# Twenty subtractions between two layers: who makes them, and when

## The chip, the cores and the metric

The kernel runs on one core of one Trainium2 chip. The metric is the device time of one execution in microseconds; a kernel's time is the median of its runs. The core's engines work side by side, each through its own queue in order, and wait for each other by semaphores: TensorE (PE; PEld is its weight load), VectorE (DVE), ScalarE (ACT), GpSimd (POOL), and SyncE (SP), which issues the transfers.

## The reference, cut to what matters

Attention with two kinds of windows makes x (2304 tokens by 512), and two layers follow:

```python
def _moe_ref(x, w_gate, w_val, w_out):       # first layer, inner width 1536
    g = x @ w_gate
    silu = g * (1.0 / (1.0 + np.exp(-g)))
    val = x @ w_val
    return (silu * val @ w_out).astype(np.float32)

def _moe2_ref(x, w1, w2, w3, w_out):         # second layer, inner width 1024
    a = x @ w1
    b = x @ w2
    h = a * b @ w3
    return (h @ w_out).astype(np.float32)
```

The weights come as 64-bit floats. The output of the first layer is the x of the second, and the change is about that hand-over.

## The kernel before

Every product is made from two parts of each operand. A float32 value v is split into hi, its rounding to float32r, and lo = v - hi; a product is then three matmuls (hi hi, hi lo, lo hi). For x these are the tiles `x_hi` and `x_lo`, one of each per group of tokens, with the 512 rows of x in four parts of 128 (kk, or cc where they are written). The 2304 tokens are five groups g = 0 to 4: four of 512 and a short one of 256.

After the attention stage the program is a list of 100 steps (c, g): chunks c = 0 to 11 are the first layer (128 inner columns each), c = 12 to 19 the second, and in each chunk the five groups follow one another. The order of a step is the order of the code, on every engine:

- `up_mm(c, g)` (L540): TensorE makes pa and then pb, 12 matmuls each, two products of x with the chunk's weights. `up_product` (L526) puts the matmuls that read `x_lo` at places 3, 7, 11 and 12 of the twelve; the last reads part 3 of `x_lo`.
- `up_act` (L557): ScalarE makes ga from pa (silu in the first layer, a copy in the second), VectorE pr = pb * ga (L613), ScalarE sh, the hi part of pr (L620), GpSimd sl = pr - sh (L621).
- `down` of the step before (`down1` L703 for the first layer, `down2` L728 for the second): TensorE multiplies sh and sl of the previous step by the output weights, four results of three matmuls in four PSUM banks po0 to po3, and VectorE adds each to the running sum (y in the first layer, o in the second, L701; the first time it copies, L699). A bank's next use waits until VectorE has read it.
- for g = 4, from chunk 11 on, `fold_mm` (L750): 24 matmuls that multiply w3 by the output weights.
- the weight jobs of the step (`next_job`): VectorE turns 64-bit weights into float32 with five instructions (L125 to L135, the tiles val_w), for w3 also a transpose (L180); ScalarE takes the hi part (L191, for w3 L183, w3h) and GpSimd subtracts (L192, for w3 L184, w3l). Chunk 11 has jobs in steps (11,0) and (11,1), chunk 12 in (12,0) to (12,3): two of w3, then two of the next chunk's weights.

In chunk 11 `down1` finishes y, and there x for the second layer is made: after each addition ScalarE writes `x_hi` (L722), and a subtraction makes `x_lo` (L726), for parts 0 and 2 on GpSimd, for 1 and 3 on VectorE. Parts 0 to 2 are subtracted when the following part has been added. Both write with a stride, as the second layer takes the tokens in another order. The first reader of group g of these tiles is `up_mm(12, g)`; `down1(11, g)` is issued in the step behind (11, g), and `up_mm(12, g)` four steps later.

Before the list of steps, the attention stage runs with its own order; the change doesn't touch it.

Of the kernel before, what the change touches and what calls it, by code (L numbers as in the profile page):

```python
# [9 lines left out]
F32 = mybir.dt.float32  # L10
# [4 lines left out]
ALU = mybir.AluOpType  # L15
# [19 lines left out]
def attention_ffn_kernel(  # L35
# [14 lines left out]
    nc = tc.nc  # L50
# [4 lines left out]
    KT = DM // P  # L55
# [3 lines left out]
    NFT = FF // P  # L59
# [4 lines left out]
    groups = []  # L64
    t0 = 0
    while t0 < NT:
        n = min(512, NT - t0)
# [14 lines left out]
    def tokens(x, kk, t0, n):  # L82
        a = t0 - t0 % 512
        assert t0 + n <= a + 512
        return x[a // 512][:, kk, t0 - a:t0 - a + n]
# [20 lines left out]
    def bank(tag, name, bufs):  # L106
        return ps.tile([P, 512], F32, tag=tag, name=name, bufs=bufs)
# [88 lines left out]
    def jobs_of(c):  # L196

        res = [[] for _ in groups]
        if c + 1 < NCH:
            first = 1  # L200
            if c == NFT - 2:

                res[0].append(("w3", 0, 0))
                res[4].append(("w3", 0, 1))
            if c == NFT - 1:
                first = 0
            if NFT <= c:
                f = c + 1 - NFT
                res[0].append(("w3", f, 0))
                res[1].append(("w3", f, 1))  # L210
                first = 2
            if c == 0:

                res[4].append(("w", 1, 2))
            else:
                for j in range(3 if c + 1 < NFT else 2):
                    res[first + j].append(("w", c + 1, j))
        if 1 <= c <= NJ:
            res[4].append(("wo", c - 1, 0))
        return res  # L220
# [22 lines left out]
    def next_job():  # L243

        while not next(running):
            pass
# [279 lines left out]
    def up_product(c, g, j, pt):  # L526

        t0, n = groups[g]
        hi, lo = whl[c]

        terms = [(a, x, kk) for kk in range(KT) for a, x in ((hi, x_hi), (lo, x_hi))]
        for kk in range(KT):
            terms.insert(min(4 * kk + 2, len(terms)), (hi, x_lo, kk))
        for i, (a, x, kk) in enumerate(terms):
            ws = slice((j * KT + kk) * P, (j * KT + kk + 1) * P)
            nc.tensor.matmul(out=pt[:, :n], lhsT=a[:, ws], rhs=tokens(x, kk, t0, n),  # L536
                             start=i == 0, stop=i == len(terms) - 1)
            yield

    def up_mm(c, g):  # L540
        pa = bank("pa", f"pa{c}_{g}", 2)
        pb = bank("pb", f"pb{c}_{g}", 2)
        for j, pt in enumerate((pa, pb)):
            for _ in up_product(c, g, j, pt):
                pass
        upp[c, g] = pa, pb

    def up_gate(c, g, pa):
        n = groups[g][1]
        ga = sp.tile([P, 512], F32, tag="ga", name=f"ga{c}_{g}", bufs=2)  # L550
        if c < NFT:
            nc.scalar.activation(out=ga[:, :n], in_=pa[:, :n], func=AF.Silu)
        else:
            nc.scalar.copy(out=ga[:, :n], in_=pa[:, :n])
        return ga

    def up_act(c, g):  # L557
        pa, pb = upp.pop((c, g))
        up_val(c, g, up_gate(c, g, pa), pb)
# [50 lines left out]
    def up_val(c, g, ga, pb):  # L610
        n = groups[g][1]
        pr = sp.tile([P, 512], F32, tag="pr", name=f"pr{c}_{g}", bufs=2)
        nc.vector.tensor_tensor(out=pr[:, :n], in0=pb[:, :n], in1=ga[:, :n], op=ALU.mult)  # L613
        split_act(c, g, pr)
# [82 lines left out]
    def accumulate(dst, src, first):  # L697
        if first:
            nc.vector.tensor_copy(out=dst, in_=src)  # L699
        else:  # L700
            nc.vector.tensor_tensor(out=dst, in0=src, in1=dst, op=ALU.add)  # L701

    def down1(c, g):  # L703

        t0, n = groups[g]
        hi, lo = whl[c]
        sh, sl = st.pop((c, g))
        if c == 0:
            acc[g] = yp.tile([P, KT, n], F32, tag=f"acc{g}", name=f"y{g}")
        y = acc[g]  # L710
        rest = []
        for cc in range(KT):
            ws = slice(2 * PW + cc * P, 2 * PW + (cc + 1) * P)
            po = bank(f"po{cc}", f"po{c}_{g}_{cc}", 1)
            for a, x, first, last in ((hi, sh, True, False), (hi, sl, False, False), (lo, sh, False, True)):
                nc.tensor.matmul(out=po[:, :n], lhsT=a[:, ws], rhs=x[:, :n], start=first, stop=last)  # L716
            accumulate(y[:, cc, :], po[:, :n], c == 0)
            if c == NFT - 1:

                xh, xl = (tokens(x, cc, t0, n).rearrange("p (a m r) -> p a r m", m=QB, r=DIL) for x in (x_hi, x_lo))  # L720
                yc = y[:, cc, :].rearrange("p (a r m) -> p a r m", m=QB, r=DIL)
                nc.scalar.copy(out=xh, in_=yc)  # L722
                rest.append((cc, xl, yc, xh.bitcast(F32)))
            while rest and (cc == KT - 1 or rest[0][0] < cc):
                i, xl, yc, xh = rest.pop(0)
                (nc.vector if i % 2 else nc.gpsimd).tensor_tensor(out=xl, in0=yc, in1=xh, op=ALU.subtract)  # L726

    def down2(c, g):  # L728

# [16 lines left out]
    def down(c, g):  # L746
        (down1 if c < NFT else down2)(c, g)


    def fold_mm(f):  # L750
        pt = bank("pa", f"fold{f}", 2)
        for j in range(NJ):
            hi, lo = w3T[f, j // HJ]
            for a, b, first, last in ((hi, wo_hi, True, False), (hi, wo_lo, False, False), (lo, wo_hi, False, True)):
                nc.tensor.matmul(out=pt, lhsT=a[:, j % HJ * P:(j % HJ + 1) * P], rhs=b[:, j, :],  # L755
                                 start=first and j == 0, stop=last and j == NJ - 1)
        hi, lo = (t[:, 2 * PW:WC] for t in slice_tiles(NFT + f))
        nc.scalar.copy(out=hi, in_=pt)
        nc.vector.tensor_tensor(out=lo, in0=pt, in1=hi.bitcast(F32), op=ALU.subtract)

    for n, (c, g) in enumerate(steps):
        if n >= 2:
            if n >= GFILL:
                up_mm(c, g)
            up_act(c, g)
        if n >= 1:
            down(*steps[n - 1])
        f = c + 1 - NFT
        if 0 <= f < NF2:
            if g == 4:  # L770
                fold_mm(f)
        for _ in jobs_of(c)[g]:
            next_job()
# [31 lines left out]
```

## Time and profile before

| what | us |
|---|---|
| median of 3 runs | 884.83 (884.32 to 885.89) |
| the profiled execution | 883.91 |
| its span, first to last instruction | 882.1 |
| TensorE busy | 865.2 (98%) |
| VectorE busy | 605.6 (69%) |
| GpSimd busy | 300.5 (34%) |
| ScalarE busy | 249.7 (28%) |

All times in rows are microseconds from the start of the span. A windows row has, for one stretch, its length, then for PE, PEld, DVE, ACT and POOL the busy time and the number of instructions, then the granted TensorE clock as a share of full speed, the share of time that the DMA engines moved data, and GB/s. A timeline row has the start, the time taken, engine, line, operation, the tiles it writes and reads, shapes, and how many like instructions were merged into it; in brackets stands the time that the engine had been idle before it, and what ended that. Matmuls overlap in their pipeline, so their pace is read from start to start, not from the time that one takes. An instruction that is held up while it executes shows a longer time, not an idle one. A row of a line's summary gives the least, the median and the greatest time of one in ns. A chain row has start, time, engine, tile, line and count of merged instructions.

### The profile page before, as it was taken

How to read it: one execution, taken by the hardware profiler on the slowest of the kernel's cores; microseconds unless marked ns; L12 is line 12 of the kernel's file. 1: busy time of each engine (PE TensorE's matmuls, PEld its weight loads, DVE VectorE, ACT ScalarE, POOL GpSimd, SP SyncE). 2: the span in 40 equal slices, each digit the busy share in tenths (PEclk: the TensorE clock that was granted, in tenths of full speed). 3: DMA queues.
4: the chain of work that ended last, by engine and by line, in shares of the span. 5: the costliest groups of instructions: out<-in, count | busy, mean ns of one | idle time of the engine just before them, and what ended most of it. 6: DMA issues, size and time to landing. Idle time of an engine off the chain costs nothing.

```text
span 882.1 us, 13481 instructions
## 1 busy us (share of the span) xinstructions
PE 865.2 (98%) x5192; PEld 722.0 (82%) x5192; DVE 605.6 (69%) x1078; ACT 249.7 (28%) x503; POOL 300.5 (34%) x296
## 2 busy tenths in 40 slices
PE   8899999999999999999999999999999999999998
PEld 5678778888888888888888887888888888888886
DVE  6898876676766767666677766767574757575725
ACT  5788521212222112221122256212121212121211
POOL 7676522322323223232232354323131323131311
PEclk9999999999999999999999999999999999999999
DMA  7998401211212112121121220112121212120014
GB/s 190 228 178 195 124 28 45 72 49 48 71 48 72 49 48 72 48 72 48 48 72 38 69 61 1 50 47 60 37 68 45 55 50 63 32 73 25 1 48 166
DMA packets 105551, 61.70 MB, mean 70 GB/s; under 512 B 71696, under 2 KB 100624, under 8 KB 105488
## 3 DMA queue, kind: packets, MB, share of 16 engines
q1 hardware_dynamic: 104944, 60.58, 25.5%
q8 instruction: 41, 0.67, 0.3%
q10 hardware_dynamic: 544, 0.26, 0.1%
q14 instruction: 22, 0.18, 0.1%
HBM read 56.10 MB, written 4.72 MB: 69 GB/s over the span
## 4 chain that ended last, share of the span: by engine, by line
PE 86%; DVE 9%; ACT 2%; issue 1%; DMA 1%; POOL 1%; SPq 0%; DVEq 0%; ACTq 0%; POOLq 0%
PE pa L536 26%; PE pb L536 26%; PE po L716 15%; PE po L741 11%; PE fold L755 5%; DVE mx L442 1%; DVE s L436 1%; ACT x_hi L722 1%; DVE mx L452 1%; DMA raw_w<-in_moe_w_gate_dram 1%; DVE x_lo L726 1%; DVE x_lo L518 1%; PE pp L470 1%; PE av L500 1%; DVE val_w L132 1%
## 5 line engine op out<-in xcount | busy, mean ns | idle before, releaser
L613 DVE TENSOR_TENSOR pr<-pb,ga 128x512 f32<-128x512 f32 (+1 forms) x98 | 62.4, 637 | 206.0 <-PE pb L536 99.7
L621 POOL TENSOR_TENSOR sl<-pr,sh 128x512 fp32r<-128x512 f32 (+1 forms) x98 | 115.9, 1183 | 240.3 <-ACT sh L620 239.7
L536 PE MATMUL pa<-x_hi,whi 128*128 128x512 f32 (+1 forms) x392 | 143.7, 369 | 0.0
L536 PE MATMUL pa<-x_hi,wlo 128*128 128x512 f32 (+1 forms) x392 | 143.5, 368 | 0.0
L536 PE MATMUL pb<-x_hi,whi 128*128 128x512 f32 (+1 forms) x392 | 143.2, 367 | 0.0
L536 PE MATMUL pb<-x_hi,wlo 128*128 128x512 f32 (+1 forms) x392 | 143.2, 367 | 0.0
L192 POOL TENSOR_TENSOR wlo<-val_w,whi 128x512 fp32r<-128x512 f32 x52 | 67.3, 1294 | 193.4 <-ACT whi L191 193.3
L701 DVE TENSOR_TENSOR y<-po,y 128x512 f32<-128x512 f32 (+1 forms) x220 | 131.5, 632 | 0.0
L536 PE MATMUL pb<-x_lo,whi 128*128 128x512 f32 (+1 forms) x392 | 128.4, 368 | 0.0
L536 PE MATMUL pa<-x_lo,whi 128*128 128x512 f32 (+1 forms) x392 | 128.2, 368 | 0.0
L620 ACT CAST sh<-pr 128x512 fp32r<-128x512 f32 (+1 forms) x98 | 56.8, 580 | 149.3 <-DVE pr L613 145.8
L191 ACT CAST whi<-val_w 128x512 fp32r<-128x512 f32 x52 | 32.3, 622 | 227.1 <-DVE val_w L135 227.1
L716 PE MATMUL po<-sh,whi 128*128 128x512 f32 (+1 forms) x240 | 88.7, 369 | 1.4 <-DVE y L701 1.1
L716 PE MATMUL po<-sl,whi 128*128 128x512 f32 (+1 forms) x240 | 88.7, 369 | 1.4 <-POOL sl L621 1.4
L716 PE MATMUL po<-sh,wlo 128*128 128x512 f32 (+1 forms) x240 | 88.3, 368 | 0.0
L536 PEld LDWEIGHTS pa<-x_hi,whi 128*128 128x128 f32 x392 | 73.9, 188 | 12.7
L536 PEld LDWEIGHTS pa<-x_hi,wlo 128*128 128x128 f32 x392 | 73.9, 188 | 12.6
L536 PEld LDWEIGHTS pb<-x_hi,wlo 128*128 128x128 f32 x392 | 73.9, 189 | 12.2
L536 PEld LDWEIGHTS pb<-x_hi,whi 128*128 128x128 f32 x392 | 73.9, 189 | 12.2
L536 PEld LDWEIGHTS pa<-x_lo,whi 128*128 128x128 f32 x392 | 72.4, 188 | 12.4
L536 PEld LDWEIGHTS pb<-x_lo,whi 128*128 128x128 f32 x392 | 72.5, 189 | 12.1
L701 DVE TENSOR_TENSOR o<-po,o 128x512 f32<-128x512 f32 x126 | 81.3, 685 | 0.2 <-PE po L741 0.2
(108 smaller groups left out, 1351.9 us busy)
## 6 DMA issues: line engine op xcount, KB each, us to landing
raw_w<-in_moe_w_dram SPq DMA_DIRECT2D x256, 32.0 KB, 1.8
raw_w<-in_moe_w_dram SPq DMA_DIRECT2D x16, 512.0 KB, 3.5
raw_w<-in_moe_w_gate_dram SPq DMA_DIRECT2D x12, 512.0 KB, 3.7
raw_w<-in_moe_w_val_dram SPq DMA_DIRECT2D x12, 512.0 KB, 3.6
raw_w<-in_moe_w_out_dram SPq DMA_DIRECT2D x12, 512.0 KB, 3.5
out_dram<-o SPq DMA_DIRECT2D x18, 256.0 KB, 2.1
raw_wo<-in_moe_w_out_dram SPq DMA_DIRECT2D x8, 512.0 KB, 3.5
vnear<-in_v_dram SPq DMA_DIRECT2D x32, 96.0 KB, 4.4
```

The source lines that it names most:

```text
L132: nc.vector.scalar_tensor_tensor(out=b, in0=up, scalar=-0x40000000, in1=b, op0=ALU.bitwise_and, op1=ALU.bitwise_or)
L191: nc.scalar.copy(out=hi, in_=val)
L192: nc.gpsimd.tensor_tensor(out=lo, in0=val, in1=hi.bitcast(F32), op=ALU.subtract)
L436: nc.vector.tensor_tensor(out=s.rearrange("q (t u) c -> q t u c", u=2), in0=sc.pop((u, par)).rearrange("q (t u) c -> q t u c", u=2), in1=m ...
L536: nc.tensor.matmul(out=pt[:, :n], lhsT=a[:, ws], rhs=tokens(x, kk, t0, n), start=i == 0, stop=i == len(terms) - 1)
L613: nc.vector.tensor_tensor(out=pr[:, :n], in0=pb[:, :n], in1=ga[:, :n], op=ALU.mult)
L620: nc.scalar.copy(out=sh[:, :n], in_=pr[:, :n])
L621: nc.gpsimd.tensor_tensor(out=sl[:, :n], in0=pr[:, :n], in1=sh[:, :n].bitcast(F32), op=ALU.subtract)
L701: nc.vector.tensor_tensor(out=dst, in0=src, in1=dst, op=ALU.add)
L716: nc.tensor.matmul(out=po[:, :n], lhsT=a[:, ws], rhs=x[:, :n], start=first, stop=last)
L741: nc.tensor.matmul(out=po, lhsT=x[:, ts], rhs=a[:, ws], start=first, stop=last)
L755: nc.tensor.matmul(out=pt, lhsT=a[:, j % HJ * P:(j % HJ + 1) * P], rhs=b[:, j, :], start=first and j == 0, stop=last and j == NJ - 1)
```

## The change

All twenty subtractions become GpSimd's. `down1` no longer issues them: it makes four additions, then four `x_hi`, and appends the four subtractions to a list `low`. A new function `low_parts(n)` takes n from the front of the list. It is called once a step, right after `up_act`, and so stands in GpSimd's queue behind that step's sl: three in the steps of chunk 11, one in the short group's step, four in the steps of chunk 12 until the list is empty.

```diff
@@ -708,22 +708,27 @@
         if c == 0:
             acc[g] = yp.tile([P, KT, n], F32, tag=f"acc{g}", name=f"y{g}")
         y = acc[g]
-        rest = []
         for cc in range(KT):
             ws = slice(2 * PW + cc * P, 2 * PW + (cc + 1) * P)
             po = bank(f"po{cc}", f"po{c}_{g}_{cc}", 1)
             for a, x, first, last in ((hi, sh, True, False), (hi, sl, False, False), (lo, sh, False, True)):
                 nc.tensor.matmul(out=po[:, :n], lhsT=a[:, ws], rhs=x[:, :n], start=first, stop=last)
             accumulate(y[:, cc, :], po[:, :n], c == 0)
-            if c == NFT - 1:
-
+        if c == NFT - 1:
+
+            for cc in range(KT):
                 xh, xl = (tokens(x, cc, t0, n).rearrange("p (a m r) -> p a r m", m=QB, r=DIL) for x in (x_hi, x_lo))
                 yc = y[:, cc, :].rearrange("p (a r m) -> p a r m", m=QB, r=DIL)
                 nc.scalar.copy(out=xh, in_=yc)
-                rest.append((cc, xl, yc, xh.bitcast(F32)))
-            while rest and (cc == KT - 1 or rest[0][0] < cc):
-                i, xl, yc, xh = rest.pop(0)
-                (nc.vector if i % 2 else nc.gpsimd).tensor_tensor(out=xl, in0=yc, in1=xh, op=ALU.subtract)
+                low.append((g, xl, yc, xh.bitcast(F32)))
+
+
+    low = []
+
+    def low_parts(n):
+        for _ in range(min(n, len(low))):
+            _, xl, yc, xh = low.pop(0)
+            nc.gpsimd.tensor_tensor(out=xl, in0=yc, in1=xh, op=ALU.subtract)
 
     def down2(c, g):
 
@@ -761,8 +766,10 @@
     for n, (c, g) in enumerate(steps):
         if n >= 2:
             if n >= GFILL:
+                assert not any(l[0] == g for l in low)
                 up_mm(c, g)
             up_act(c, g)
+            low_parts(4 if c == NFT else 1 if g == len(groups) - 1 else 3)
         if n >= 1:
             down(*steps[n - 1])
         f = c + 1 - NFT
```

GpSimd's queue of the kernel before, from sl of step (12,0) to the first weight job of step (12,2). The number behind sl is its group, x_lo_75 to x_lo_78 are the tiles of groups 1 to 4, and x2 is two like instructions in a row:

```order
L621 TENSOR_TENSOR sl_0_5844<-pr_0_5841,sh_0_5843 128x512
L726 TENSOR_TENSOR x_lo_78<-y_2307,x_hi_73 128x4x64 x2
L184 TENSOR_TENSOR w3l_0_5886<-w3t_0_5883,w3h_0_5885 128x512
L621 TENSOR_TENSOR sl_1_5920<-pr_1_5917,sh_1_5919 128x512
L184 TENSOR_TENSOR w3l_1_5955<-w3t_1_5952,w3h_1_5954 128x512
L621 TENSOR_TENSOR sl_2_5989<-pr_2_5986,sh_2_5988 128x512
L192 TENSOR_TENSOR wlo_6037<-val_w_0_6030,whi_6036 128x512
```

The two subtractions of the short group are the last of the ten. The same place after the change:

```order
L621 TENSOR_TENSOR sl_0_5835<-pr_0_5832,sh_0_5834 128x512
L731 TENSOR_TENSOR x_lo_75<-y_2158,x_hi_70 128x2x4x64
L731 TENSOR_TENSOR x_lo_76<-y_2187,x_hi_71 128x2x4x64 x3
L184 TENSOR_TENSOR w3l_0_5877<-w3t_0_5874,w3h_0_5876 128x512
L621 TENSOR_TENSOR sl_1_5911<-pr_1_5908,sh_1_5910 128x512
L731 TENSOR_TENSOR x_lo_76<-y_2187,x_hi_71 128x2x4x64
L731 TENSOR_TENSOR x_lo_77<-y_2242,x_hi_72 128x2x4x64 x3
L184 TENSOR_TENSOR w3l_1_5950<-w3t_1_5947,w3h_1_5949 128x512
L621 TENSOR_TENSOR sl_2_5984<-pr_2_5981,sh_2_5983 128x512
L731 TENSOR_TENSOR x_lo_77<-y_2242,x_hi_72 128x2x4x64
L731 TENSOR_TENSOR x_lo_78<-y_2307,x_hi_73 128x4x64 x3
L192 TENSOR_TENSOR wlo_6036<-val_w_0_6029,whi_6035 128x512
```

Where two stood, twelve stand, with a thirteenth behind sl of step (12,3), and the last one of a group stands behind sl of the step that comes just before the group's `up_mm`.

VectorE's queue of the kernel before from pr of step (11,2) to pr of (11,3); y_2158 is y of group 1:

```order
L613 TENSOR_TENSOR pr_2_5628<-pb_2_5601,ga_2_5626 128x512
L701 TENSOR_TENSOR y_2158<-po_1_0_5634,y_2158 128x512
L701 TENSOR_TENSOR y_2158<-po_1_1_5640,y_2158 128x512
L701 TENSOR_TENSOR y_2158<-po_1_2_5647,y_2158 128x512
L726 TENSOR_TENSOR x_lo_75<-y_2158,x_hi_70 128x2x4x64
L701 TENSOR_TENSOR y_2158<-po_1_3_5654,y_2158 128x512
L726 TENSOR_TENSOR x_lo_75<-y_2158,x_hi_70 128x2x4x64
L613 TENSOR_TENSOR pr_3_5690<-pb_3_5663,ga_3_5688 128x512
```

Each subtraction on VectorE stands where the fourth addition, or the next pr, comes behind it. After the change:

```order
L613 TENSOR_TENSOR pr_2_5624<-pb_2_5597,ga_2_5622 128x512
L701 TENSOR_TENSOR y_2158<-po_1_0_5633,y_2158 128x512
L701 TENSOR_TENSOR y_2158<-po_1_1_5638,y_2158 128x512
L701 TENSOR_TENSOR y_2158<-po_1_2_5643,y_2158 128x512
L701 TENSOR_TENSOR y_2158<-po_1_3_5648,y_2158 128x512
L613 TENSOR_TENSOR pr_3_5685<-pb_3_5658,ga_3_5683 128x512
```

The two subtractions are gone from between pr, the four additions and the next pr.

## Rows read from the trace of the kernel before

**Rows 1.** Busy time by stretch, 552 to 870 us.

```profile
552.00:870.00 318.00, 318.00 (x1480) 266.07 (x1479) 199.84 (x336) 62.23 (x112) 81.27 (x67) 1.00 0.18 49
```

**Rows 2.** Timeline of TensorE, 527 to 537 us.

```profile
527.93 0.39 PE L716 MATMUL po<-sh,wlo 128*128 128x512 f32 x1
528.52 0.50 PE L716 MATMUL po<-sh,whi 128*128 128x512 f32 x1 [0.21 <-DVE y L701]
528.86 0.39 PE L716 MATMUL po<-sl,whi 128*128 128x512 f32 x1
...
532.18 0.40 PE L716 MATMUL po<-sh,whi 128*128 128x512 f32 x1
533.44 0.50 PE L716 MATMUL po<-sl,whi 128*128 128x512 f32 x1 [0.85 <-POOL sl L621]
...
535.15 0.39 PE L716 MATMUL po<-sh,wlo 128*128 128x512 f32 x1
536.47 0.50 PE L716 MATMUL po<-sh,whi 128*128 128x512 f32 x1 [0.93 <-DVE y L701]
```

**Rows 3.** Timeline of VectorE, 523 to 531 us, down1 of group 1.

```profile
523.29 1.87 DVE L701 TENSOR_TENSOR y<-po,y 128x512 f32<-128x512 f32 x3
526.12 1.75 DVE L726 TENSOR_TENSOR x_lo<-y,x_hi 128x512 fp32r<-128x512 f32 x1 [0.95 <-ACT x_hi L722]
...
529.66 1.11 DVE L726 TENSOR_TENSOR x_lo<-y,x_hi 128x512 fp32r<-128x512 f32 x1 [1.20 <-ACT x_hi L722]
530.68 0.68 DVE L613 TENSOR_TENSOR pr<-pb,ga 128x512 f32<-128x512 f32 x1
```

**Rows 4.** Timeline of GpSimd, 524 to 533 us.

```profile
524.11 1.30 POOL L621 TENSOR_TENSOR sl<-pr,sh 128x512 fp32r<-128x512 f32 x1 [0.64 <-ACT sh L620]
525.37 1.57 POOL L726 TENSOR_TENSOR x_lo<-y,x_hi 128x512 fp32r<-128x512 f32 x1
...
532.10 1.28 POOL L621 TENSOR_TENSOR sl<-pr,sh 128x512 fp32r<-128x512 f32 x1 [2.81 <-ACT sh L620]
```

**Rows 5.** Chain that ended last, 542 to 558 us.

```profile
542.91 2.76 PE pa L536 x12
...
548.40 1.43 PE po L716 x12
...
555.30 2.72 PE po L741 x12
```

**Rows 6.** Summary of line 726 on GpSimd.

```profile
L726 POOL TENSOR_TENSOR x_lo<-y,x_hi x10: 862/1584/2232, 513.4 to 552.5; 128x512 fp32r<-128x512 f32 x8, 128x256 fp32r<-128x256 f32 x2
```

**Rows 7.** Timeline of ScalarE, 557 to 558 us, step (12,1).

```profile
557.27 0.62 ACT L183 CAST w3h<-w3t 128x512 fp32r<-128x512 f32 x1 [4.50 <-DVE w3t L180]
557.80 0.58 ACT L554 COPY ga<-pa 128x512 f32<-128x512 f32 x1
```

**Rows 8.** Timeline of VectorE, 553 to 559 us, a w3 job and pr.

```profile
554.15 0.43 DVE L127 TENSOR_SCALAR val_w<-val_w 128x512 f32<-128x512 f32 x1
...
556.53 0.71 DVE L180 STREAM_TRANSPOSE w3t<-val_w 128x512 f32<-128x512 f32 x1
558.47 0.69 DVE L613 TENSOR_TENSOR pr<-pb,ga 128x512 f32<-128x512 f32 x1 [1.23 <-ACT ga L554]
```

**Rows 9.** Timeline of VectorE, conversions that meet GpSimd, 52 to 111 us.

```profile
52.72 1.20 DVE L132 SCALAR_TENSOR_TENSOR val_w<-raw_w,val_w 128x512 int32<-128x512 int32 x1
...
107.73 1.38 DVE L127 TENSOR_SCALAR val_w<-val_w 128x512 f32<-128x512 f32 x1
109.15 1.40 DVE L129 TENSOR_SCALAR val_w<-val_w 128x512 int32<-128x512 int32 x1
```

**Rows 10.** Timeline of GpSimd, 51 to 111 us.

```profile
51.58 1.79 POOL L443 TENSOR_TENSOR s<-s,mx 128x384 f32<-128x384 f32 x2
...
107.43 1.40 POOL L621 TENSOR_TENSOR sl<-kept,sh 128x512 fp32r<-128x512 f32 x1 [3.07 <-ACT sh L620]
108.79 1.48 POOL L192 TENSOR_TENSOR wlo<-val_w,whi 128x512 fp32r<-128x512 f32 x1
```

## The prediction

> **What bounds the kernel now.** I began with the busy time by stretch: from 552 us on TensorE has no idle time at all [rows 1], so only its own waits can be won there, and the change adds none of its instructions and takes none away. Next I read TensorE's timeline around 500 to 552 us, where down1 of chunk 11 runs. Its matmuls start 0.23 us apart, and three starts there are late [rows 2]: by 0.59 - 0.23 = 0.36, 1.26 - 0.23 = 1.03 and 1.32 - 0.23 = 1.09 us. The matmul behind a wait comes 0.34 instead of 0.23 us later, 0.11 each. Together 2.8 us, and that is everything a perfect change could return.
>
> VectorE's timeline shows where the waits come from. Its own subtraction stands between the third and fourth y, waits 0.95 us for ScalarE's x_hi and takes 1.75 us; the fourth y, for which TensorE's bank waits, comes after that, and the next subtraction puts off pr of the next group [rows 3]. With pr late, sh and sl are late, and TensorE waits for sl [rows 2, 4].
>
> **What goes.** Ten subtractions leave VectorE. Behind pr then stand four y in a row (0.62 us each) [rows 3], and down1 has nothing to wait for: no y and no pr stands behind a subtraction any more. All three late starts should go: -2.8 us. TensorE would begin up_mm(12,0) at 542.9 - 2.8 = 540.1 instead of 542.9 us [rows 5].
>
> **What comes.** GpSimd has twenty subtractions instead of ten: 1.57 us each for 512 tokens, 0.86 for 256 (the smallest in the line's summary) [rows 4, 6]. What matters is when. In steps (11,2) to (11,4) only seven are queued. Thirteen are left for chunk 12, whose up_mm reads these very tiles: the last subtraction of groups 1, 2, 3 and 4 stands directly behind sl of the step before the group's up_mm. Its reader is the last matmul of pa, 11 x 0.23 = 2.5 us after pa begins. So the chain pr 0.69, sh 0.62 (a ScalarE copy of w3h's shape), sl 1.28, subtraction 1.57 [rows 4, 7, 8] = 4.2 us must fit between the end of pb and that matmul. TensorE does the down product in that time, 2.72 us [rows 5], plus 2.5: 5.2 us. Slack 1.0 us where pr starts as pb ends. For group 1 the down product is that of the short group, 1.43 us [rows 5]: 3.9 us, no slack.
>
> pr does not start as pb ends. In the kernel before, pr(12,1) begins 3 us after pb's end, held up by the chain conversion, transpose, w3h, ga [rows 7, 8]; nobody minded, since sl was needed a whole step later. Now that delay goes straight to the last subtraction. And it grows, because the conversions now run beside the queue of subtractions. The trace shows what that does: L127 takes 1.38 us beside sl instead of 0.43 and ends 0.28 us after sl; the next, L129, then waits out the wlo that had been queued, 1.40 us, again to 0.28 us behind its end; L132 ends 0.55 us behind the GpSimd operation it meets [rows 9, 10]. In turn wlo ends 1.16 us after L127 and not 1.29: it had waited too. So the two engines take turns, one instruction each. y reads PSUM and is not touched: three take 1.87 us though sl starts beside the second [rows 3, 4]; pr reads PSUM too.
>
> The Trainium skill, page "SBUF — State Buffer", section "Who interferes with whom", says that a VectorE instruction in a 2-port mode or with two SBUF inputs and a GpSimd instruction exclude one another for a whole instruction. The trace agrees for L127 to L132 (1.38 and 1.20 us); without that rule the sum below would be the first rival, with it the sum as it stands. The page leaves open which of two full queues goes next; the turns are this trace's.
>
> Working through it, with a subtraction at 1.44 us behind a conversion (1.57 less the 0.13 that wlo lost in the same place):
> - Step (12,0): pb ends 545.6, pr 546.3, sh 546.9, sl 548.2. The conversion of the w3 job starts during sl and ends at 548.5; the last subtraction of group 1 ends at 549.9. TensorE wants it at 545.6 + 1.43 + 2.5 = 549.5: with the signal's way a wait of about 0.6.
> - The other four conversions take turns with three subtractions of group 2: L127 ends at 550.2, then subtraction 551.6, L129 551.9, subtraction 553.35, L132 553.9, subtraction 555.35, L135 555.9. Transpose 0.71, w3h 0.62, ga 0.58, pr 0.69, sh 0.62, sl 1.28, subtraction 1.57 end at 562.1. TensorE, 0.6 late, wants it at 558.05: a wait of 4.05.
> - Step (12,1): o copies after pr (558.6) to 561.1, five conversions against the last subtraction of group 2 and three of group 3 to 568.5, the same chain behind them to 574.65. TensorE, resumed at 562.1, wants it at 562.35 + 2.7 + 2.75 + 2.5 = 570.3: a wait of 4.35.
> - Step (12,2): the subtractions are the short group's (0.86), the chain has a whi in place of transpose and w3h, and ends at 583.7. TensorE's matmuls for 256 tokens start 0.12 apart, so it wants the tile at 574.9 + 2.7 + 2.75 + 1.3 = 581.65: a wait of 2.05.
> - From (12,4) on the queue is empty and nothing reads x_lo late; the wait is not given back, since TensorE is the bound [rows 1].
>
> Waits 0.6 + 4.05 + 4.35 + 2.05 = 11.05, and 4 x 0.11 for starting again: +11.5. With -2.8: +8.7 us. The profiled execution took 883.9 us (span 882.1), so 892.6; the median of the three runs is 0.9 us above it, which would make 893.5. I say 893.0.
>
> Where the trace is silent: it has no queue of four subtractions beside five conversions. One end is that conversions are not held up at all, the other that they get no turn until the queue is empty; both are below. The transpose beside GpSimd is not seen either; in this walk it meets none, and against one sl it would cost at most 1.3 us, at least nothing. ScalarE's x_hi, now four in a row, end about 4 us after the first and are off the path.
>
> **The rivals.**
> First, no exclusion for these forms, GpSimd's queue alone: in (12,0) and (12,1) it has sl 1.28, four subtractions 6.3 and w3l (as sl) 1.28 = 8.9 us against TensorE's step of 3 x 2.72 = 8.16. The last subtractions come about 0.5, 0.7 and 0.7 us late, with restarts 2.2: -0.6 us, 883.3. For it: both engines' work would fit. Against: [rows 9, 10]. Chance 0.09.
>
> Second, the change does what it is written to do and no wait comes in: -2.8 us, 881.1. This needs the chain of 4.2 us to start within 1 us of pb's end, against the 3 us of the kernel before. Chance 0.04.
>
> Third, VectorE goes first and makes its five conversions in one go, the subtractions behind them. The last one of group 1 then ends near 552.6, a wait of 3.1, but the chain behind is short and the next two waits are about 0.7: 4.5 + 0.3 - 2.8 = +2.0, 885.9. Against: L129 had to wait for wlo though L127 had just run. Chance 0.07.
>
> Fourth, VectorE gets no turn while subtractions are queued: per step the conversions end some 1.0 us later than with turns, +2.9 in three steps, 896.5. Against: L127 ran between sl and wlo. Chance 0.12.
>
> Fifth, the turns with the clock on top. The waits of before [rows 2] were at most 1.1 us, and the stretch behind them has a granted clock of 1.00 [rows 1]; those forecast are four times as long. Were the clock to fall to 1.2 GHz, the 12 matmuls of pb and 12 of po behind a wait would take up to 5.4 us more; after the second wait that is mostly hidden in the third (4.35), after the third only 2.05 are hidden, so up to 3.4 us more: 896. Chance 0.10. The Trainium skill's page "TensorE: Matmul & The Clock Gate" says in "What's actually happening" that an idle TensorE goes back to the half clock; no row here shows it in the middle of the work.
>
> **How the numbers follow.** The forecast with turns has 0.58, within 891 to 895 (each of the four waits is uncertain by some 0.5 us), the fifth rival 0.10 and the fourth 0.12 above it. 888 to 897 leaves out the first three rivals, 0.20 together. What can be told from no change is 0.2%, 1.8 us. Faster by more: the second rival and a sliver of the first, 0.05. Within: the rest of the first and a little of the third, 0.09. Slower: 0.86.
>
> **What would show it.** In the new profile TensorE should wait four times, on the last matmul of pa for GpSimd's subtraction, in (12,1) to (12,4), the middle two longest; the waits for y and sl near 528 to 536 us should be gone; L125 to L129 in (12,0) and (12,1) should take about 1.7 us. Conversions at 0.43 us there would prove me wrong about the turns; no wait of pa would prove wrong the chain behind pr.

## The result, and the profile after

The changed kernel takes 892.73 us (median of 6 runs, 892.32 to 894.25), the kernel before 884.25 in the same comparison: 8.5 us more, a ratio of 1.0096 with a 95% interval of 1.0083 to 1.0109. The forecast was 893.0 us. The profiled execution has a span of 891.1 us against 882.1. Medians here and below are of runs at full clock; two of the six runs of the early drain below were at a granted clock of 0.75 and 0.56, in 1074.72 and 1440.86 us, and are left out of its median.

Three rows of the chain that ended last give the account (start, time, engine, tile, line, count):

```profile
540.41 2.76 PE pa L536 x12
...
583.44 0.83 POOL x_lo L731
...
588.88 5.50 PE fold L760 x24
```

pa of step (12,0) starts at 540.41 us; before it was 542.91 [rows 5]. The steps in front of chunk 11's end run 0.29 us later here than before (pa of (11,1) starts at 504.78 against 504.49), so TensorE has won 2.8 us in between. The fold of step (12,4) starts at 588.88, before at 579.96: 8.9 us later. So 11.4 us are lost between the two.

VectorE's timeline of the changed kernel shows what was won in its first row, four y in one piece of 2.71 us, where a subtraction stood before the fourth [rows 3], and what was lost in the others, the conversions of step (12,0), the transpose behind them, the next pr and the first conversion of step (12,1):

```profile
519.15 2.71 DVE L701 TENSOR_TENSOR y<-po,y 128x512 f32<-128x512 f32 x4
...
547.96 1.07 DVE L125 TENSOR_SCALAR val_w<-raw_w 128x512 int32<-128x512 int32 x1
549.07 1.64 DVE L127 TENSOR_SCALAR val_w<-val_w 128x512 f32<-128x512 f32 x1
550.74 1.65 DVE L129 TENSOR_SCALAR val_w<-val_w 128x512 int32<-128x512 int32 x1
552.42 1.91 DVE L132 SCALAR_TENSOR_TENSOR val_w<-raw_w,val_w 128x512 int32<-128x512 int32 x1
554.37 1.92 DVE L135 SCALAR_TENSOR_TENSOR val_w<-raw_w,val_w 128x512 int32<-128x512 int32 x1
556.33 0.71 DVE L180 STREAM_TRANSPOSE w3t<-val_w 128x512 f32<-128x512 f32 x1
558.27 0.69 DVE L613 TENSOR_TENSOR pr<-pb,ga 128x512 f32<-128x512 f32 x1 [1.23 <-ACT ga L554]
...
561.27 1.45 DVE L125 TENSOR_SCALAR val_w<-raw_w 128x512 int32<-128x512 int32 x1
```

L127 and L129 take 1.65 us instead of 0.43 [rows 8], L132 1.91. GpSimd at the same time: sl of (12,0) and behind it the last subtraction of group 1 and three of group 2, then the same in (12,1), one group on, and the subtractions of (12,2) and (12,3):

```profile
547.45 1.30 POOL L621 TENSOR_TENSOR sl<-pr,sh 128x512 fp32r<-128x512 f32 x1 [11.16 <-ACT sh L620]
548.71 7.04 POOL L731 TENSOR_TENSOR x_lo<-y,x_hi 128x512 fp32r<-128x512 f32 x4
...
559.69 1.26 POOL L621 TENSOR_TENSOR sl<-pr,sh 128x512 fp32r<-128x512 f32 x1 [0.63 <-ACT sh L620]
560.91 6.63 POOL L731 TENSOR_TENSOR x_lo<-y,x_hi 128x512 fp32r<-128x512 f32 x4
...
573.49 4.74 POOL L731 TENSOR_TENSOR x_lo<-y,x_hi 128x512 fp32r<-128x512 f32 x4
...
583.40 0.86 POOL L731 TENSOR_TENSOR x_lo<-y,x_hi 128x256 fp32r<-128x256 f32 x1
```

Four subtractions take 7.04 us here, 1.76 each, against 1.57 [rows 4] and 1.53 beside transposes (the experiment below): the two engines take turns, and each pays for it. The last subtraction of group 2 is the first of the four that start at 560.91, behind sl, behind pr (558.27). TensorE's timeline shows the readers, the last matmul of pa in steps (12,1) to (12,4), each under the matmul before it:

```profile
549.45 0.39 PE L536 MATMUL pa<-x_lo,whi 128*128 128x512 f32 x1
550.49 0.50 PE L536 MATMUL pa<-x_lo,whi 128*128 128x512 f32 x1 [0.64 <-POOL x_lo L731]
...
558.57 0.39 PE L536 MATMUL pa<-x_lo,whi 128*128 128x512 f32 x1
562.49 0.79 PE L536 MATMUL pa<-x_lo,whi 128*128 128x512 f32 x1 [3.53 <-POOL x_lo L731]
...
563.51 0.63 PE L536 MATMUL pb<-x_hi,wlo 128*128 128x512 f32 x1
...
571.96 0.39 PE L536 MATMUL pa<-x_lo,whi 128*128 128x512 f32 x1
575.07 0.50 PE L536 MATMUL pa<-x_lo,whi 128*128 128x512 f32 x1 [2.72 <-POOL x_lo L731]
...
583.65 0.28 PE L536 MATMUL pa<-x_lo,whi 128*128 128x256 f32 x1
584.32 0.39 PE L536 MATMUL pa<-x_lo,whi 128*128 128x256 f32 x1 [0.38 <-POOL x_lo L731]
```

From start to start, less one matmul, they are late by 0.81, 3.69, 2.88 and 0.55 us, 7.9 together; the three waits of before are gone. Behind the second and the third wait the matmuls start 0.43 us apart instead of 0.23 (563.08 and 563.51 are two that follow one another). The windows view has the granted clock of those two stretches (the last but two of its columns):

```profile
562.07:565.48 3.41, 2.99 (x7) 2.41 (x8) 3.34 (x3) 0.00 (x0) 3.41 (x3) 0.50 0.03 5
575.72:579.13 3.41, 3.41 (x10) 2.63 (x9) 3.31 (x4) 0.00 (x0) 2.51 (x3) 0.50 0.14 31
```

0.50 is 1.2 GHz. From the wait's end to the eleventh matmul of the next pa, 562.49 to 571.96, TensorE needs 9.47 us for what takes 35 x 0.227 = 7.9 at full clock, and 575.07 to 583.65 is 8.58 for 6.9: 3.2 us more for the clock, restarts included. 7.9 + 3.2 and the restarts of the first and the last wait, 0.1 each, make 11.3 of the 11.4.

### The profile page after: what moved, and what is told of

Same layout as the page of the kernel before. It is cut to its first block, busy times and chain, and to the rows that moved or that the text cites. A ratio compares the mean times of both kernels' runs of the same rounds, so it can differ in the third digit from the quotient of the medians.

```text
span 891.1 us, 13483 instructions
## 1 busy us (share of the span) xinstructions
PE 868.0 (97%) x5192; PEld 724.2 (81%) x5192; DVE 607.2 (68%) x1068; ACT 248.6 (28%) x503; POOL 313.2 (35%) x306
## 4 chain that ended last, share of the span: by engine, by line
PE 87%; DVE 10%; issue 1%; POOL 1%; DMA 1%; SPq 0%; ACT 0%; DVEq 0%; POOLq 0%; ACTq 0%
PE pb L536 26%; PE pa L536 26%; PE po L715 16%; PE po L746 10%; PE fold L760 5%; DVE mx L442 1%; PE av L500 1%; DVE val_w L132 1%; DVE s L436 1%; PE pp L470 1%; DVE mx L452 1%; DVE val_w L127 1%; DMA raw_w<-in_moe_w_gate_dram 1%; PE sc L427 1%; DVE val_w L129 1%
```

## The experiments

My theory had two parts: freeing VectorE gives 2.8 us, and the late place of the last subtractions, behind a chain of conversions that take turns with GpSimd, costs 11. The rivals were GpSimd's queue by its length alone, conversions that cost by themselves, and the clock.

**GpSimd alone, nothing put off.** In the kernel before:

```diff
-                (nc.vector if i % 2 else nc.gpsimd).tensor_tensor(out=xl, ...)
+                nc.gpsimd.tensor_tensor(out=xl, ...)
```

> The kernel before with one edit: all four subtractions of a group are GpSimd's, each at its old place in the code, none put off. It is the part of the change that frees VectorE, alone. My theory: the three late starts near 528 to 536 us go (-2.8); the conversions of step (11,1) now meet four subtractions and put pr(11,2) some 4 us later than without, which may bring a wait of about 1 us for sl of (11,3): 881.5 to 882.7. Rival (taking subtractions from VectorE is itself the loss): slower than before, 886 or more.

Measured: 882.21 us against 884.51, ratio 0.9975 (0.9965 to 0.9986). Of TensorE's waits from 500 to 610 us one is left (the view of waits: line waited for, us in total, times, longest):

```profile
PE po L716 <- POOL sl L621: 0.6, 1, 0.6
```

The freed VectorE is a gain: 2.3 us are left of the 2.8, and the wait for sl of (11,3) that was expected is there. So the loss of the change comes with the putting off.

**Drained early.** In the changed kernel four subtractions a step, and groups 3 and 4 directly behind their own down1:

```diff
-            low_parts(4 if c == NFT else 1 if g == len(groups) - 1 else 3)
+            low_parts(4)
         if n >= 1:
             down(*steps[n - 1])
+            if (c, g) in ((NFT - 1, len(groups) - 1), (NFT, 0)):
+                low_parts(4)
```

> All twenty subtractions on GpSimd as in the changed kernel, but four of them behind each step's sl in chunk 11, groups 3 and 4 directly behind their own down1, so that none is left for the step before its reader. My theory (the late place costs 11.4 us, the freed VectorE gives 2.8): no wait of TensorE is left between 505 and 600 us, 2.8 us under the kernel before, 881.5. Rival (GpSimd is too slow for all twenty wherever they stand): waits for sl come instead, 884 or more.

Measured: 881.24 against 884.51, ratio 0.9961 (0.9949 to 0.9974). The same kernel again, now with its profile:

> The version with an early drain once more, for a profile at full clock: 881.2 us within 0.6, and in it no wait of TensorE between 505 and 600 us; conversions of (12,0) at about 1.1 us each beside the four subtractions of the short group, with nothing waiting for them. Rival: a wait for sl of (12,1) or for the subtractions of group 3, some 0.5 us, stands there and was hidden in the median.

881.41 against 884.66, ratio 0.9964 (0.9951 to 0.9976). TensorE, first column behind the length, has no idle time in the stretch:

```profile
505.00:600.00 95.00, 95.00 (x447) 79.41 (x446) 61.69 (x100) 35.35 (x52) 50.92 (x39) 1.00 0.17 44
```

That is the 2.8 us with nothing given back, a little more in the median, and both kernels beaten. GpSimd is not too slow for the twenty subtractions. But the expected conversions of 1.1 us are not there. VectorE from (12,0) on:

```profile
547.78 5.22 DVE L125 TENSOR_SCALAR val_w<-raw_w 128x512 int32<-128x512 int32 x1
553.03 0.43 DVE L127 TENSOR_SCALAR val_w<-val_w 128x512 f32<-128x512 f32 x1
```

and GpSimd, from sl of (11,3) on without a break, with eight subtractions, sl and four more at the end:

```profile
527.96 1.31 POOL L621 TENSOR_TENSOR sl<-pr,sh 128x512 fp32r<-128x512 f32 x1 [0.79 <-ACT sh L620]
...
536.00 12.19 POOL L731 TENSOR_TENSOR x_lo<-y,x_hi 128x512 fp32r<-128x512 f32 x8
548.05 1.37 POOL L621 TENSOR_TENSOR sl<-pr,sh 128x512 fp32r<-128x512 f32 x1
549.30 3.42 POOL L731 TENSOR_TENSOR x_lo<-y,x_hi 128x256 fp32r<-128x256 f32 x4
```

L125 takes 5.22 us and ends at 553.00, 0.28 us behind the last subtraction (552.72). Here VectorE got no turn in five changes of instruction on GpSimd. That was my fourth rival's behaviour, which I had set aside because L127 once ran between sl and wlo [rows 9, 10].

**Four in every step.** Only the number in `low_parts` is changed:

```diff
-            low_parts(4 if c == NFT else 1 if g == len(groups) - 1 else 3)
+            low_parts(4)
```

> One number changed in the changed kernel: four subtractions in every step. Group 3 then stands in step (12,0), two steps ahead of its reader, group 4 in (12,1), and both still beside conversions. My theory: the conversions take 1.7 us each in (12,0) as before, pr(12,1) is as late, but nobody waits for a last subtraction; at most some 1 us of waiting for sl in (12,2): 881.5 to 882.5. Rival (conversions slowed by GpSimd cost by themselves, through VectorE's queue): about half of the changed kernel's loss stays, 888.

Measured: 884.53 against 884.51, ratio 1.0001 (0.9992 to 1.0009). It loses 2 us more than I said. TensorE's waits from 500 to 610 us:

```profile
PE po L746 <- POOL sl L621: 1.2, 2, 0.6
PE po L746 <- ACT sh L620: 0.7, 2, 0.5
```

and VectorE, a conversion beside the short group's subtractions, and pr of (12,2):

```profile
563.50 0.98 DVE L127 TENSOR_SCALAR val_w<-val_w 128x512 f32<-128x512 f32 x1
...
569.48 0.69 DVE L613 TENSOR_TENSOR pr<-pb,ga 128x512 f32<-128x512 f32 x1 [1.17 <-ACT ga L554]
```

No last subtraction is waited for, and that alone takes 8.2 us off the changed kernel. But two steps in a row with slow conversions, 0.98 us even beside the short subtractions, put pr(12,2) at 569.48 and its sh and sl behind the matmuls that want them. The rival had a point: slow conversions do cost something by themselves, near 2.9 us here with restarts, of the 6 it asked for.

**Transposes for conversions.** In the changed kernel, for the jobs of steps (12,0) to (12,2):

```diff
-        yield from to_f32(val, raw_of.pop(job))
+        if job in (("w3", 1, 0), ("w3", 1, 1), ("w", NFT + 1, 0)):
+            up = raw_of.pop(job).rearrange("p (n t) -> p n t", t=2)[:, :, 1].bitcast(F32)
+            for _ in range(4):
+                nc.vector.transpose(out=val, in_=up)
+                yield
+        else:
+            yield from to_f32(val, raw_of.pop(job))
```

> The changed kernel with the five conversions of the three weight jobs in steps (12,0) to (12,2) left out and four 128x512 transposes of 0.71 us put in their place (2.84 us against 2.83): the weights of those jobs are not converted. If a transpose, with one SBUF input, does not wait for GpSimd, this is GpSimd's queue without turns: the waits of TensorE shrink from 7.9 to about 2 us, 883.7, which was the first rival's price. If my theory of turns is wrong and the length of GpSimd's queue alone makes the waits, the time stays near 892. If transposes take turns too (each about 2 us), it stays near 891 and tells only that.

Measured: 883.21 against 884.51, ratio 0.9985 (0.9976 to 0.9994). VectorE and GpSimd in (12,0):

```profile
547.67 2.94 DVE L180 STREAM_TRANSPOSE val_w<-raw_w 128x512 f32<-128x512 f32 x4
550.65 0.71 DVE L186 STREAM_TRANSPOSE w3t<-val_w 128x512 f32<-128x512 f32 x1
553.42 0.69 DVE L619 TENSOR_TENSOR pr<-pb,ga 128x512 f32<-128x512 f32 x1 [2.06 <-PE pb L542]
```

```profile
547.16 1.31 POOL L627 TENSOR_TENSOR sl<-pr,sh 128x512 fp32r<-128x512 f32 x1 [11.24 <-ACT sh L626]
548.42 6.12 POOL L737 TENSOR_TENSOR x_lo<-y,x_hi 128x512 fp32r<-128x512 f32 x4
```

Four transposes take 2.94 us, 0.71 each, in the middle of the subtractions, and the subtractions 1.53 each. With the same queues, the same places and the same busy time on VectorE, but without turns, pr(12,1) stands at 553.42 instead of 558.27 and 9.5 us of the time are gone. So the turns make the loss; what the length of GpSimd's queue does by itself is to make the last matmuls of pa 0.65, 0.28 and 0.23 us late in steps (12,1) to (12,3), in sum less than the first rival's 0.5, 0.7 and 0.7. The first late start of the changed kernel, 0.81 us, is therefore mostly that length; the later ones come from the turns.

**A busy TensorE.** In the changed kernel, ahead of the last matmul of pa:

```diff
-            for _ in up_product(c, g, j, pt):
-                pass
+            for i, _ in enumerate(up_product(c, g, j, pt)):
+                if j == 0 and i == 3 * KT - 2:
+                    for _ in range({(NFT, 2): 14, (NFT, 3): 11}.get((c, g), 0)):
+                        nc.tensor.matmul(out=pb, lhsT=whl[c][0][:, 0:P], rhs=tokens(x_hi, 0, *groups[g]),
+                                         start=True, stop=True)
```

> The changed kernel with 14 and 11 additional matmuls (into the bank of pb, which is empty then) ahead of the late last matmul of pa in steps (12,2) and (12,3), so that TensorE is busy in most of the two long waits. Their own time, 25 x 0.23 = 5.7 us, lies inside the waits. If the clock then stays at 2.4 GHz: by my theory the chain on VectorE, ScalarE and GpSimd sets the end and the time lost at 1.2 GHz lay in front of the next wait, so the total stays, 892.7 within 0.5. Rival (the lower clock costs what its matmuls took longer, 3.2 us): 889.5.

Measured: 894.75 us, ratio to the kernel before 1.0125 (1.0108 to 1.0142): neither of the two, 2.0 us more than without. The readers in TensorE's timeline, and two stretches of the windows view:

```profile
562.53 0.50 PE L536 MATMUL pa<-x_lo,whi 128*128 128x512 f32 x1 [0.42 <-POOL x_lo L734]
...
575.13 0.50 PE L536 MATMUL pa<-x_lo,whi 128*128 128x512 f32 x1 [1.65 <-POOL x_lo L734]
...
584.16 0.39 PE L536 MATMUL pa<-x_lo,whi 128*128 128x256 f32 x1 [1.75 <-POOL x_lo L734]
```

```profile
556.00:582.00 26.00, 23.93 (x108) 19.32 (x108) 21.96 (x26) 5.18 (x9) 17.56 (x13) 1.00 0.18 45
585.50:588.90 3.40, 3.40 (x11) 2.82 (x11) 2.30 (x5) 1.30 (x3) 1.41 (x2) 0.50 0.42 102
```

The clock stayed at full speed to 582 us, and the last reader starts at 584.16, with the lower clock it was 584.32. So the 3.2 us at 1.2 GHz cost the changed kernel nothing: they lay in front of a later wait. But now the clock falls behind the last wait, from 585.5 to 588.9 us, where no wait takes it in; from the last reader to the fold it is 6.15 us (584.16 to 590.31) instead of 4.56. That explains 1.6 of the 2.0 us; the rest lies within the intervals.

**Turns or no turns.** Two kernels with the same eight subtractions behind sl of (12,0), beside the same conversions. In the first GpSimd has nothing to do for 5 us before that sl; in the second, groups 1 and 2 stand there. The first:

```diff
-            low_parts(4 if c == NFT else 1 if g == len(groups) - 1 else 3)
+            low_parts(4)
         if n >= 1:
             down(*steps[n - 1])
+            if (c, g) in ((NFT, 0),):
+                low_parts(4)
```

> Early drain with another split: groups 0, 1, 2 behind sl of (11,2), (11,3), (11,4), and eight subtractions (groups 3 and 4) behind sl of (12,0), beside the same conversions. GpSimd has nothing from about 542 to 547 us, so its row is broken before sl(12,0). If turns are always taken: conversions of 1.7 us, pr(12,1) near 559, sl(12,1) near 561.5 behind the subtractions, a wait of some 0.5 us: 882.0. If VectorE gets no turn whenever GpSimd has many queued: as the next kernel, 885 to 887.

The second:

```diff
-            low_parts(4 if c == NFT else 1 if g == len(groups) - 1 else 3)
+            low_parts(4 if n > (NFT - 1) * len(groups) + 2 else 0)
         if n >= 1:
             down(*steps[n - 1])
+            if (c, g) in ((NFT - 1, len(groups) - 1), (NFT, 0)):
+                low_parts(4)
```

> The same eight subtractions behind sl(12,0) beside the same conversions, but groups 1 and 2 now stand directly before that sl, so that GpSimd's row runs from about 529 to 559 us without a break (as in the early drain, where L125 took 5.2 us and ended 0.28 us behind the last subtraction). If a row without a break gives VectorE no turn: L125 lasts from 548 to 559, pr(12,1) comes near 564, and TensorE waits 4 to 5 us for sl(12,1): 885.5 to 887. If turns are taken here too: as the kernel beside it, 882 to 883.

Measured: 883.19 against 884.28, ratio 0.9983 (0.9973 to 0.9993), and 888.20, ratio 1.0038 (1.0023 to 1.0053). Both are about 1.2 us above what I had given, 882.0 and 885.5 to 887. VectorE and GpSimd of the first:

```profile
547.67 1.07 DVE L125 TENSOR_SCALAR val_w<-raw_w 128x512 int32<-128x512 int32 x1
548.78 1.67 DVE L127 TENSOR_SCALAR val_w<-val_w 128x512 f32<-128x512 f32 x1
```

```profile
547.16 1.30 POOL L621 TENSOR_TENSOR sl<-pr,sh 128x512 fp32r<-128x512 f32 x1 [5.17 <-ACT sh L620]
548.42 10.88 POOL L731 TENSOR_TENSOR x_lo<-y,x_hi 128x512 fp32r<-128x512 f32 x8
```

and of the second:

```profile
548.08 11.23 DVE L125 TENSOR_SCALAR val_w<-raw_w 128x512 int32<-128x512 int32 x1
```

```profile
548.40 1.29 POOL L621 TENSOR_TENSOR sl<-pr,sh 128x512 fp32r<-128x512 f32 x1
549.66 9.36 POOL L731 TENSOR_TENSOR x_lo<-y,x_hi 128x512 fp32r<-128x512 f32 x8
```

In the first, L125 gets its turn at once and so does each conversion behind it. In the second, L125 takes 11.23 us and ends at 559.31, 0.29 behind the last of eight subtractions (559.02); pr comes at 563.65, and TensorE is 4.2 us late for sh of (12,1). Its waits from 500 to 610 us, and the windows view of the twelve matmuls of po behind this wait:

```profile
PE po L746 <- ACT sh L620: 4.0, 1, 4.0
```

```profile
565.08:570.83 5.75, 5.63 (x13) 3.95 (x13) 4.93 (x9) 0.54 (x2) 1.26 (x1) 0.50 0.04 8
```

At a granted clock of 0.50 the twelve take 5.75 us instead of 2.72, a restart and a short wait for sl included. No later wait takes these 3.0 us in: 4.2 + 3.0 is about what this kernel is behind the early drain, 7.0. My 885.5 to 887 had no term for the clock. The first kernel has two waits for sl, 1.0 us of idle time, where I had counted one of 0.5. So the same work is 5 us apart by whether GpSimd's row was broken before it, about half of it through the late pr and half through the clock that fell in that wait.

## Why the prediction was right

The gain. Three late starts, 2.8 us: measured 2.8, and the two kernels that keep the gain and lose little, the early drain and GpSimd in place, show it in the time.

The late chain. Set 0.29 us back for the earlier difference, the last subtractions end at 562.1, 574.7 and 584.0 us; forecast were 562.1, 574.65 and 583.7. The turns are as read in the trace of before, where two conversions took 1.38 and 1.40 us; beside the longer subtractions they take 1.65 and 1.92, and about 1.7 was forecast. The transposes show that they are the cause, since without them 9.5 us go away.

The sum of the waits. This term was mis-sized: 11.05 forecast, 7.9 measured. The clock fell behind the second and the third wait, TensorE came 1.5 and 1.7 us later to the next one, and the waits of 4.35 and 2.05 became 2.88 and 0.55. The total didn't move, because the end was set by the chain and not by TensorE: 7.9 + 3.2 for the clock is what had been put down as waits alone. The fifth rival, the turns with the clock on top, so had its mechanism right; its up to 5.4 us behind the third wait were 1.7, less than the 2.05 that were to hide them. That the sum could do without the clock was luck in part: where no later wait takes the fall in, it costs 1.6 us (the busy TensorE) or 3.0 (the unbroken row).

The rivals. The first (no exclusion) and the second (a free gain) are the transposes and the early drain: both times, 883.21 and 881.24, are near those given, 883.3 and 881.1, but in kernels in which the turns, or the late readers, had been taken out. Against the kernel before, measured beside them, they gain 1.3 and 3.3 us where 0.6 and 2.8 were given. The third (all five conversions in one go) is false: L127, the second of them, took 1.64 us. The fourth (no turn while GpSimd has work queued) is false for the changed kernel, and true for others.

## What to carry to other kernels

Work that is put off to another engine's queue is placed by its reader: count back from the matmul that reads it through everything that stands before it in order, here conversion, transpose, copy, activation, product and split. Before moving an operation to GpSimd, look in the trace for VectorE rows that read 0.43 us alone and 1.4 beside it, since a queue with room may still hold up its neighbour. The best place is where that neighbour has little to do: with sixteen of the twenty subtractions queued in chunk 11 and four in step (12,0) the change gains 3.3 us, with seven in chunk 11 and thirteen in chunk 12 it loses 8.5.

## What was not expected of the hardware

VectorE is not always given its turn. Beside a row of GpSimd instructions that had run for some 20 us without a break, one conversion took 5.22 us, and in another kernel 11.23 us, past five and nine further GpSimd instructions, and ended 0.28 and 0.29 us after the last. With the row broken before its first instruction, it went in after that one, at 1.07 us, and in turns from there on. The kind of instruction under way as VectorE arrives doesn't decide it alone: in both cases without a turn VectorE came during a subtraction, but in step (12,1) of the changed kernel too (561.27, the subtraction had begun at 560.91), and there it went in after that one, at 1.45 us. In that case GpSimd's row was 1.6 us old, in the two others 20. That the length of the row decides is likely but not shown: no run has a row of a length in between with more queued behind it as VectorE comes.

A transpose of 128x512 takes 0.71 us beside sl and the subtractions as alone, twelve of twelve, so it can be put where a conversion can't.

The clock fell to 1.2 GHz for 3.4 us at the end of a wait of 3.69 us in which TensorE did nothing, and again behind one of 2.88; with matmuls in most of those two waits it stayed at 2.4 GHz there, and fell behind the next one. Why it fell there, behind a wait of 1.75 us, no run shows.
